# One float16 cast and one subtraction for two key tiles (1536 columns) in a block-sparse attention kernel

## The chip, the cores and the metric

The kernel runs on one core of one Trainium2 chip. The metric is the device time of one execution in microseconds (us). The kernel before was timed three times: 983.65, 980.24 and 983.49 us, median 983.49 us.

The engines are named as in the profile: PE (TensorE, matmuls) with PEld (its weight loads), DVE (VectorE), ACT (ScalarE), POOL (GpSimd), SP (SyncE, which issues every DMA of this kernel).

## The reference, cut to what matters

```python
scores = scale * np.matmul(q, k.transpose(0, 1, 3, 2))      # 4 x 8 heads, 768 tokens, 64 wide
...
scores = np.where(mask, scores, -1000000000.0)              # blocks of 32: window, ends, 3 sampled
scores = scores - np.max(scores, axis=-1, keepdims=True)
attn = np.exp(scores)
attn = attn / (np.sum(attn, axis=-1, keepdims=True) + 1e-09)
out = np.matmul(attn, v)
...
h = x @ w_in                                                # x: 3072 x 512, w_in: 512 x 2048
g = h - np.tanh(h)
return (g @ w_out).astype(np.float32)
```

## The kernel before, in words

The 32 heads are worked on in 16 pairs, as two heads fill 128 partitions. A head has six key tiles of 128 keys. Three pairs' worth of transposed q and k stand in three slots of SBUF (slot0 to slot2).

For each head and key tile, the attention part does these steps:

- **smax**, two heads ahead: PE computes plain scores into a PSUM tile `sm`, DVE takes their row maximum (`mc`, L259). After six tiles PE turns the maxima (`pmt`, L264), DVE scales them (`nm`, L266), and a DMA puts them as a row into the slot, so that the next step's matmuls subtract them.
- **qk_exp**: PE computes the scores of all 768 queries against 128 keys into a PSUM tile `st` (L283, L284); ACT writes their exponential into an SBUF tile `pe` (L287).
- **split**: the exponential becomes two float16 parts. `ph` is the cast of `pe` (on ACT, L297, or on DVE, L295); `pl` is `pe - ph` (on POOL or DVE, L299).
- **accum**: PE multiplies `ph` and `pl` with the values' two parts into a PSUM tile `av` (L313, L321, L322; 18 matmuls per tile). The two tiles of a pair of key tiles (0 and 1, 2 and 3, 4 and 5) are accumulated one behind the other, and the first is ordered behind the subtraction of the second.
- **norm**: DVE divides by the row sums (L331, L334, L335).

Once per pair of heads, **prep_qk** prepares a later pair: PE transposes k and q into PSUM tiles `ptk` and `ptq`, ACT writes the high parts `hik`, `hiq` (L200), DVE the low parts `lok`, `loq` (L201), and DMAs spread them into a slot (L213). **prep_v** splits the values (`am`, `pa`, `sb`, then `vhl` on ACT L240 and DVE L241). This falls into the odd heads. The PSUM tiles `st`, `sm`, `ptk` and `ptq` share three buffers (`big`); `av`, `pa` and `pmt` share two others. The feed-forward part follows from about 434 us on and is not touched.

All steps are written as events with a time in units of key tiles, sorted by it. A scheduler then makes each engine's order and hands out the buffers by its own estimate of when they come free, so durations that it expects change both. From head 5 on, `in_order` fixes the order of the `st`, `sm` and `av` matmuls on PE.

`load_pre` and `convert_pre` load six weight tiles (`raw...`, tag `wraw`, two buffers) during the attention, convert them on DVE (`cvti`, `cvto`; L436, L439, L442) and store them to DRAM (`wi`, `wo`).

Which casts and subtractions go to DVE stands in small tables by the tile's number modulo 12: casts 4 and 10, subtraction 11, and in the last heads casts 0, 2, 4, 6, 8, 10 and subtractions 2, 5, 8, 11. `pe` has four buffers, `ph` and `pl` eight each.

Of the kernel before, what the change touches and what calls it, by code (L numbers as in the profile page):

```python
# [11 lines left out]
F32 = mybir.dt.float32  # L12
# [10 lines left out]
P = 128  # L23
# [20 lines left out]
NV = 3  # L44
PH_DVE_END = (0, 2, 4, 6, 8, 10)
TF, NMH = 2, 2
TV0 = -4
PAIR = 0.99
PB = 8
XF = 8  # L50
# [8 lines left out]
RS, RQ, RV, HR = 1, 2.5, 3, 6  # L59
PL_DVE = (11,)  # L60
PL_DVE_END = (2, 5, 8, 11)
PH_DVE = (4, 10)

# [43 lines left out]
def attention(ctx, tc, q, k, v, samp, w_in, w_out, blocks, xscr, ident, ps, slots, wt, f2, ffn):  # L107
# [44 lines left out]
    def setup():  # L152
# [17 lines left out]
        nc.vector.tensor_scalar(out=neg[R, :], in0=allow, scalar1=1.0, scalar2=-MASKED, op0=ALU.subtract, op1=ALU.mult)  # L170
        nat = p2.tile([P, S], F32, tag="pe", name="nat", bufs=4)
        mk = p2.tile([P, S], F32, tag="pe", name="mk", bufs=4)
        nc.vector.tensor_copy(
# [102 lines left out]
    def qk_exp(h, kt):  # L276
# [8 lines left out]
        in_order(h, ms[0], ms[-1])  # L285
        pe = p2.tile([P, S], F32, tag="pe", name=f"pe{h}_{kt}", bufs=4)
        nc.scalar.activation(out=pe, in_=st[:, 0:S], func=AF.Exp, scale=0.125)  # L287
        pes[h, kt] = pe

    def split(h, kt):  # L290
        pe = pes.pop((h, kt))
        ph = p2.tile([P, S], F16, tag="ph", name=f"ph{h}_{kt}", bufs=PB)
        pl = p2.tile([P, S], F16, tag="pl", name=f"pl{h}_{kt}", bufs=PB)
        if (h * T + kt) % 12 in (PH_DVE if h < HPH else PH_DVE_END):
            nc.vector.tensor_copy(out=ph, in_=pe)  # L295
        else:
            nc.scalar.activation(out=ph, in_=pe, func=AF.Copy)  # L297
        eng = nc.vector if (h * T + kt) % 12 in (PL_DVE if h < HPL else PL_DVE_END) else nc.gpsimd
        d = eng.tensor_tensor(out=pl, in0=pe, in1=ph, op=ALU.subtract)  # L299
        plin[h, kt] = d  # L300
        phs[h, kt] = ph, pl

# [47 lines left out]
    def at(time, f, *args):  # L350
        ev.append((time, len(ev), f, args))
# [24 lines left out]
    def load_pre(m, ft):  # L376
        wraw[m, ft] = p2.tile([P, 1024], I32, tag="wraw", name=f"raw{m}{ft}")
        d = load_w(nc, wraw[m, ft], w_in, w_out, m, ft)
        if ft == 0:
            after(2, d)  # L380
# [7 lines left out]
    for h in range(2 * NPAIR):  # L388
        tsm = TSM + ramp(h, RS)
        for t in range(T):  # L390
            i = 6 * h + t
            at(i + tsm, smax, h, t)
            at(i, qk_exp, h, t)
            at(i + LSP, split, h, t)
            at(i + LAV + PAIR * (1 - t % 2), accum, h, t)
# [289 lines left out]
```

## Time and profile before

| What | Value |
|---|---|
| time, three runs | 983.65, 980.24, 983.49 us; median 983.49 us |
| profiled execution | span 983.2 us; its trace gives no other time |
| busy share of the span | PE 94%, PEld 78%, DVE 75%, ACT 64%, POOL 47% |
| exponentials on ACT (L287) | 192, mean 805 ns |
| casts on ACT (L297), on DVE (L295) | 154, mean 844 ns; 38, mean 704 ns |
| subtractions on POOL, on DVE (L299) | 173, mean 1692 ns; 19, mean 1455 ns |
| PE's wait for the exponential (st L283 <- ACT pe L287) | 13.4 us in 15 waits |

The exponentials run from 33.5 to 428 us of the span. Two heads take 23.5 us there: an even head some 10.5 and an odd one some 13.1. A row of a timeline has the start in us, the length in us, the engine, the line, the operation, output<-inputs, the count, and in brackets the idle time ahead of it with what ended it. A row of waits has who waited for whom, the sum in us, the number of waits and the longest.

### The profile page before, as it was taken

The page shows a single profiled execution, that of the slowest core. Times are in us where ns is not written, and L with a number is a line of the kernel's source. Part 1 is how long each engine was busy: PE and PEld are TensorE (multiplying, and loading weights), DVE is VectorE, ACT ScalarE, POOL GpSimd, SP SyncE. Part 2 cuts the span into 40 slices and gives each one's busy share as a digit, 9 for nine tenths or more (in the row PEclk, how much of TensorE's full clock was granted, in tenths as well). Part 3 has the DMA queues.
Part 4 walks back from the last instruction along what each step waited for, and adds up shares of the span by engine and source line. Part 5 has one row for each costly group of instructions (what it writes and reads, how often), then busy time and mean ns, then how long its engine had stood idle before and what let it go on. Part 6 is the DMA issues. An engine that isn't in the chain of part 4 may idle for free.

```text
span 983.2 us, 18548 instructions
## 1 busy us (share of the span) xinstructions
PE 922.6 (94%) x7264; PEld 771.1 (78%) x7264; DVE 733.4 (75%) x1119; ACT 629.7 (64%) x943; POOL 458.3 (47%) x308
## 2 busy tenths in 40 slices
PE   5788999999999999888999999999999999999997
PEld 3577788887888878767788888888888888888885
DVE  4589888887887878859999876765676666566664
ACT  1476888888888878656666665555555465555553
POOL 1365877777777777754445422222222222222221
PEclk9698999999999999898999999999999999999999
DMA  8796777676676667114451220210020000001001
GB/s 231 185 274 190 195 175 175 162 174 162 168 173 162 162 161 189 45 48 157 148 168 50 65 76 11 97 33 12 1 75 1 1 33 11 1 1 44 1 1 43
DMA packets 56263, 99.78 MB, mean 101 GB/s; under 512 B 6008, under 2 KB 26680, under 8 KB 56176
## 3 DMA queue, kind: packets, MB, share of 16 engines
q1 hardware_dynamic: 56176, 98.60, 37.0%
q8 instruction: 57, 0.93, 0.4%
q14 instruction: 30, 0.25, 0.1%
HBM read 44.64 MB, written 15.20 MB: 61 GB/s over the span
## 4 chain that ended last, share of the span: by engine, by line
PE 77%; ACT 6%; DMA 5%; DVE 5%; issue 3%; SPq 1%; POOL 1%; ACTq 0%; POOLq 0%; DVEq 0%
PE pf L537 25%; PE pf L569 8%; PE pf L570 8%; PE pf L571 8%; PE st L283 6%; PE st L284 5%; PE sm L255 5%; ACT pe L287 3%; PE av L313 2%; PE av L321 2%; PE av L322 2%; DMA slot<-lok 2%; DMA slot<-nm 2%; DVE mc L259 1%; PE pf L451 1%
## 5 line engine op out<-in xcount | busy, mean ns | idle before, releaser
L299 POOL TENSOR_TENSOR pl<-pe,ph 128x768 f16<-128x768 f32 x173 | 290.0, 1692 | 130.5 <-ACT ph L297 67.5
L560 POOL TENSOR_TENSOR gl<-t,gh 128x512 fp32r<-128x512 f32 x96 | 124.0, 1292 | 358.4 <-ACT gh L559 307.0
L259 DVE TENSOR_REDUCE mc<-sm 128x1 f32<-128x768 f32 x192 | 181.0, 951 | 53.1 <-PE sm L255 49.2
L287 ACT ACTIVATE pe<-st 128x768 f32<-128x768 f32 x192 | 154.1, 805 | 78.4 <-PE st L284 68.5
L283 PE MATMUL st<-slot 128*128 128x512 f32 (+1 forms) x384 | 146.4, 382 | 17.1 <-ACT pe L287 13.4
L552 DVE TENSOR_TENSOR t<-t,pf 128x512 f32<-128x512 f32 x94 | 64.5, 686 | 123.3 <-ACT t L546 123.2
L559 ACT ACTIVATE gh<-t 128x512 fp32r<-128x512 f32 x96 | 60.6, 632 | 120.2 <-DVE t L556 120.2
L297 ACT ACTIVATE ph<-pe 128x768 f16<-128x768 f32 x154 | 130.0, 844 | 4.7
L284 PE MATMUL st<-slot 89*128 89x512 f32 (+1 forms) x384 | 126.1, 349 | 1.0 <-DMA slot<-nm 1.0
L313 PE MATMUL av<-vhl,ph 128*128 128x65 f16 x1152 | 120.7, 195 | 0.0
L322 PE MATMUL av<-vhl,pl 128*128 128x65 f16 x1152 | 119.6, 194 | 0.9 <-POOL pl L299 0.9
L255 PE MATMUL sm<-slot 88*128 88x512 f32 (+1 forms) x384 | 111.1, 376 | 9.6 <-DMA slot<-hiq 7.0
L321 PE MATMUL av<-vhl,ph 128*128 128x64 f16 x1152 | 119.7, 196 | 0.0
L313 PEld LDWEIGHTS <-ph 128*128 128x128 f16 x1152 | 106.6, 97 | 13.6 <-issue 12.9
L322 PEld LDWEIGHTS <-pl 128*128 128x128 f16 x1152 | 107.9, 100 | 3.0 <-issue 1.5
L321 PEld LDWEIGHTS <-ph 128*128 128x128 f16 x1152 | 107.9, 98 | 0.7 <-issue 0.5
L544 ACT ACTIVATE u<-pf 128x512 f32<-128x512 f32 x94 | 56.2, 598 | 80.5 <-PE pf L537 80.2
L283 PEld LDWEIGHTS st<-slot 128*128 128x128 f32 x384 | 74.9, 195 | 35.1 <-ACT pe L287 18.5
L284 PEld LDWEIGHTS st<-slot 89*128 89x128 f32 x384 | 75.5, 197 | 11.2 <-DMA slot<-nm 2.2
L255 PEld LDWEIGHTS sm<-slot 88*128 88x128 f32 x384 | 62.6, 202 | 17.0 <-DMA slot<-mk 6.3
L570 PE MATMUL pf<-wx,gh 128*128 128x512 f32 x192 | 74.7, 389 | 0.0
L569 PE MATMUL pf<-wx,gh 128*128 128x512 f32 x192 | 74.7, 389 | 0.0
(123 smaller groups left out, 1962.8 us busy)
## 6 DMA issues: line engine op xcount, KB each, us to landing
slot<-hik SPq DMA_DIRECT2D x64, 192.0 KB
slot<-hiq SPq DMA_DIRECT2D x64, 192.0 KB
stage<-w_in SPq DMA_DIRECT2D x13, 512.0 KB
stage<-w_out SPq DMA_DIRECT2D x13, 512.0 KB
rawk<-k SPq DMA_DIRECT2D x16, 384.0 KB
rawq<-q SPq DMA_DIRECT2D x16, 384.0 KB
slot<-lok SPq DMA_DIRECT2D x32, 192.0 KB
slot<-loq SPq DMA_DIRECT2D x32, 192.0 KB
```

The source lines that it names most:

```text
L255: nc.tensor.matmul(pm[:, c], lhsT=sB[s][0:88, j, t * P : (t + 1) * P], rhs=sA[s][0:88, j, c], start=True, stop=True)
L259: maxed.append(nc.vector.tensor_reduce(out=mcs[h][:, t : t + 1], in_=pm[:, 0:S], op=ALU.max, axis=AX.X))
L283: ms.append(nc.tensor.matmul(st[:, c], lhsT=sC[s][:, j, kc], rhs=sD[s][:, j, c], start=True, stop=False))
L284: ms.append(nc.tensor.matmul(st[:, c], lhsT=sA[s][0:89, j, kc], rhs=sB[s][0:89, j, c], start=False, stop=True))
L287: nc.scalar.activation(out=pe, in_=st[:, 0:S], func=AF.Exp, scale=0.125)
L299: d = eng.tensor_tensor(out=pl, in0=pe, in1=ph, op=ALU.subtract)
L313: m = nc.tensor.matmul(o[:, t, :], lhsT=ph[:, c], rhs=vv[:, 0:65], start=(kt == 0 and t == 0), stop=False, skip_group_check=True)
L321: nc.tensor.matmul(o[:, t, 0:64], lhsT=ph[:, c], rhs=vv[:, 65:129], start=False, stop=False, skip_group_check=True)
L322: m = nc.tensor.matmul(o[:, t, :], lhsT=pl[:, c], rhs=vv[:, 0:65], start=False, stop=last, skip_group_check=True)
L537: nc.tensor.matmul(h, lhsT=w[:, cc], rhs=x[:, c, :], start=(k == 0), stop=(k == 3 * NCT - 1))
L569: nc.tensor.matmul(o, lhsT=gh[:, c], rhs=wo[0][ft], start=(ft == f0), stop=False)
L570: nc.tensor.matmul(o, lhsT=gh[:, c], rhs=wo[1][ft], start=False, stop=False)
```

## The change

Two key tiles share one `pe` tile of 1536 columns: two exponentials write its halves, and one cast and one subtraction read it whole. `ph` and `pl` get 1536 columns as well; `accum` reads their halves with the same matmuls as before. `split` is called for odd tiles alone.

The tables now count pairs of tiles modulo 6: DVE casts pair 2 (the last of an even head), and no subtraction until the last two heads, where it has pairs 1 and 5; in the last heads DVE casts pairs 0, 2 and 4. In columns the casts on DVE are as many as before; the subtraction of one tile in twelve moves from DVE to POOL. `pe` has three buffers of 1536 for four of 768, `ph` and `pl` four for eight; `wraw` has one for two.

```diff
-PH_DVE_END = (0, 2, 4, 6, 8, 10)
+PH_DVE_END = (0, 2, 4)
...
-PB = 8
+PB = 4
+NPE = 3
...
-PL_DVE = (11,)
-PL_DVE_END = (2, 5, 8, 11)
-PH_DVE = (4, 10)
+PL_DVE = ()
+PL_DVE_END = (1, 5)
+PH_DVE = (2,)
...
-        nat = p2.tile([P, S], F32, tag="pe", name="nat", bufs=4)
-        mk = p2.tile([P, S], F32, tag="pe", name="mk", bufs=4)
+        nat = p2.tile([P, S], F32, tag="pe", name="nat", bufs=NPE)
+        mk = p2.tile([P, S], F32, tag="pe", name="mk", bufs=NPE)
...
-        pe = p2.tile([P, S], F32, tag="pe", name=f"pe{h}_{kt}", bufs=4)
-        nc.scalar.activation(out=pe, in_=st[:, 0:S], func=AF.Exp, scale=0.125)
-        pes[h, kt] = pe
+        if kt % 2 == 0:
+            pes[h, kt // 2] = p2.tile([P, 2 * S], F32, tag="pe", name=f"pe{h}_{kt}", bufs=NPE)
+        nc.scalar.activation(out=pes[h, kt // 2][:, kt % 2 * S : (kt % 2 + 1) * S], in_=st[:, 0:S], func=AF.Exp, scale=0.125)
 
     def split(h, kt):
-        pe = pes.pop((h, kt))
-        ph = p2.tile([P, S], F16, tag="ph", name=f"ph{h}_{kt}", bufs=PB)
-        pl = p2.tile([P, S], F16, tag="pl", name=f"pl{h}_{kt}", bufs=PB)
-        if (h * T + kt) % 12 in (PH_DVE if h < HPH else PH_DVE_END):
+        pe = pes.pop((h, kt // 2))
+        ph = p2.tile([P, 2 * S], F16, tag="ph", name=f"ph{h}_{kt}", bufs=PB)
+        pl = p2.tile([P, 2 * S], F16, tag="pl", name=f"pl{h}_{kt}", bufs=PB)
+        n = (h * T + kt) // 2 % 6
+        if n in (PH_DVE if h < HPH else PH_DVE_END):
             nc.vector.tensor_copy(out=ph, in_=pe)
         else:
             nc.scalar.activation(out=ph, in_=pe, func=AF.Copy)
-        eng = nc.vector if (h * T + kt) % 12 in (PL_DVE if h < HPL else PL_DVE_END) else nc.gpsimd
+        eng = nc.vector if n in (PL_DVE if h < HPL else PL_DVE_END) else nc.gpsimd
         d = eng.tensor_tensor(out=pl, in0=pe, in1=ph, op=ALU.subtract)
-        plin[h, kt] = d
-        phs[h, kt] = ph, pl
+        for x in range(2):
+            plin[h, kt - 1 + x] = d
+            phs[h, kt - 1 + x] = ph[:, x * S : (x + 1) * S], pl[:, x * S : (x + 1) * S]
...
-        wraw[m, ft] = p2.tile([P, 1024], I32, tag="wraw", name=f"raw{m}{ft}")
+        wraw[m, ft] = p2.tile([P, 1024], I32, tag="wraw", name=f"raw{m}{ft}", bufs=1)
...
-            at(i + LSP, split, h, t)
+            if t % 2:
+                at(i + LSP, split, h, t)
```

The changed program's lines stand one to four lower (L255 is now L256, L287 is L289, L331 is L334).

The scheduler makes another order of it. Names in the rows below are tile, head or pair, key tile and a running number; `st19_4` is the score tile of head 19 and key tile 4, `sm21_2` the one for the maxima of head 21, `hik11` the high part of k of pair 11. All odd heads from 7 to 27 read alike.

On DVE, in the odd head 19, before:

```order
L259 TENSOR_REDUCE mc21_4748<-sm21_0_4749 128x1
L235 TENSOR_SCALAR sb10_4679<-sb10_4679 128x1
L266 TENSOR_SCALAR nm20_4702<-pmt20_4700 6x128
L238 TENSOR_SCALAR sb10_4679<-sb10_4679 128x1
L259 TENSOR_REDUCE mc21_4748<-sm21_1_4777 128x1
L201 TENSOR_TENSOR lok11_4758<-ptk11_4759,hik11_4757 128x768
L241 SCALAR_TENSOR_TENSOR vhl1_104<-rawv10_3711,sb10_4679,vhl1_104 128x12x64
L331 SCALAR_TENSOR_TENSOR rs18_4822<-av18_4615,sb9_4207 128x6
L334 RECIPROCAL rs18_4822<-rs18_4822 128x6
L259 TENSOR_REDUCE mc21_4748<-sm21_2_4850 128x1
```

and now:

```order
L260 TENSOR_REDUCE mc21_4462<-sm21_0_4463 128x1
L233 TENSOR_REDUCE sb10_4394<-pa10_4392 128x1
L236 TENSOR_SCALAR sb10_4394<-sb10_4394 128x1
L239 TENSOR_SCALAR sb10_4394<-sb10_4394 128x1
L202 TENSOR_TENSOR lok11_4468<-ptk11_4469,hik11_4467 128x768
L260 TENSOR_REDUCE mc21_4462<-sm21_1_4486 128x1
L267 TENSOR_SCALAR nm20_4416<-pmt20_4414 6x128
L334 SCALAR_TENSOR_TENSOR rs18_4531<-av18_4334,sb9_3952 128x6
L242 SCALAR_TENSOR_TENSOR vhl1_104<-rawv10_3490,sb10_4394,vhl1_104 128x12x64
L337 RECIPROCAL rs18_4531<-rs18_4531 128x6
L260 TENSOR_REDUCE mc21_4462<-sm21_2_4559 128x1
```

The low part lok11 moved ahead of the maximum over sm21_1, and nm20 behind it; between that maximum and the one over sm21_2 there stand now nm20, rs18, vhl1 and the reciprocal.

On PE, at the end of the same odd head, with the semaphores that each row waits for (the engine that signals is in the name), before:

```order
L255 MATMUL sm21_2_4850<-slot1_74 128x512 [waits DVE_49]
L255 MATMUL sm21_2_4850<-slot1_74 128x256
L283 MATMUL st19_5_4867<-slot0_73 128x512 [waits Activation_49]
L284 MATMUL st19_5_4867<-slot0_73 128x512
L283 MATMUL st19_5_4867<-slot0_73 128x256
L284 MATMUL st19_5_4867<-slot0_73 128x256
L255 MATMUL sm21_3_4874<-slot1_74 128x512 [waits DVE_49]
```

and now:

```order
L256 MATMUL sm21_2_4559<-slot1_74 128x512 [waits DVE_49]
L256 MATMUL sm21_2_4559<-slot1_74 128x256
L284 MATMUL st19_5_4572<-slot0_73 128x512 [waits DVE_49]
L285 MATMUL st19_5_4572<-slot0_73 128x512
L284 MATMUL st19_5_4572<-slot0_73 128x256
L285 MATMUL st19_5_4572<-slot0_73 128x256
L256 MATMUL sm21_3_4578<-slot1_74 128x512 [waits Activation_49]
```

The order of the matmuls is the same; the buffers are not. By the program's addresses st19_5 stood in the buffer of st19_4 (freed by ACT's exponential), and stands now in that of sm21_2 (freed by DVE's maximum); sm21_3 now takes the buffer of st19_4.

On SP, in the first heads, before:

```order
L267 DMA slot1_74<-nm2_475 1x6x128
L145 DMA rawk4_871<-k 128x768
L145 DMA rawq4_873<-q 128x768
L213 DMA slot2_75<-hik2_571 64x768 x2
L213 DMA slot2_75<-hiq2_584 64x768 x2
```

and now:

```order
L268 DMA slot1_74<-nm2_459 1x6x128
L146 DMA rawk4_830<-k 128x768
L386 DMA wi0_76<-cvti0_1794 128x512
L146 DMA rawq4_832<-q 128x768
L214 DMA slot2_75<-hik2_546 64x768 x2
L214 DMA slot2_75<-hiq2_559 64x768 x2
```

The store of the first converted weight tile (wi0), which waits for DVE's conversion, moved ahead of the load of q of pair 4 and of the DMAs that fill slot2.

## The prediction

> **What bounds the kernel now.** I read the windows by stage first, then the waits of TensorE, then the timeline around the wait that repeats.
>
> ```profile
> 33.00:106.00 73.00, 64.76 (x720) 53.92 (x720) 60.74 (x90) 50.28 (x63) 48.19 (x27) 0.88 0.79 224
> 106.00:382.00 276.00, 261.54 (x3479) 225.48 (x3475) 227.28 (x349) 229.50 (x290) 208.51 (x128) 1.00 0.67 165
> 382.00:434.00 52.00, 47.12 (x655) 40.80 (x653) 39.95 (x58) 37.66 (x53) 39.73 (x23) 0.93 0.31 85
> ```
>
> Columns: stretch, length, then busy time of PE, PEld, DVE, ACT and POOL, the granted clock, the DMA share. The change touches these three stretches alone; the feed-forward part behind 434 us runs none of its lines. In the long middle one PE is busy 95% of the time and no other engine over 84%. Time saved on ACT, DVE or POOL there is worth only the PE waits that it ends, 14.5 us at the most, and the waits view says which.
>
> ```profile
> PE st L283 <- ACT pe L287: 10.9, 12, 0.9
> PE sm L255 <- ACT pe L287: 2.4, 2, 1.4
> ```
>
> This is the window 110 to 380 us. Twelve times, once in every odd head, PE waits 0.9 us; the rest is two single waits. One of the twelve:
>
> ```profile
> 280.16 0.51 PE L255 MATMUL sm<-slot 88*128 88x512 f32 x2
> 281.61 0.50 PE L283 MATMUL st<-slot 128*128 128x512 f32 x1 [0.94 <-ACT pe L287]
> ...
> 276.96 0.79 ACT L200 ACTIVATE hik<-ptk 128x768 fp32r<-128x768 f32 x1
> 277.65 0.94 ACT L240 ACTIVATE vhl<-rawv,sb 128x768 f16<-128x768 f32 x1
> 278.49 0.79 ACT L287 ACTIVATE pe<-st 128x768 f32<-128x768 f32 x1
> 279.31 0.84 ACT L297 ACTIVATE ph<-pe 128x768 f16<-128x768 f32 x1
> 280.06 0.79 ACT L200 ACTIVATE hiq<-ptq 128x768 fp32r<-128x768 f32 x1
> 280.75 0.80 ACT L287 ACTIVATE pe<-st 128x768 f32<-128x768 f32 x1
> ```
>
> Score tile 5 of the odd head stands in the PSUM buffer of tile 4, whose exponential comes last in a full ACT queue and ends at 281.55.
>
> **The casts on ACT.** A cast of 1536 is not in the trace, so its price is bounded.
>
> ```profile
> L297 ACT ACTIVATE ph<-pe 128x768 f16<-128x768 f32 x154 | 130.0, 844 | 4.7
> L559 ACT ACTIVATE gh<-t 128x512 fp32r<-128x512 f32 x96 | 60.6, 632 | 120.2 <-DVE t L556 120.2
> ```
>
> From 512 to 768 columns the time grows by 212 ns, 0.83 ns a column; 768 more columns make 844 + 636 = 1480 ns. The ends are 844 (the single cast) and 1688 (twice it). I take 1480, the value on the line through both rows: 77 casts for 154 save 77 x 208 ns = 16 us of ACT. In even heads PE is busy throughout, so this hides behind PE. In odd heads ACT no longer sets the wait, as follows.
>
> **The odd head's wait, which stays.** The rows of the program's order above show that tile 5 (st19_5) now waits for DVE: its buffer is that of sm21_2, the matmul just ahead of it, and the maximum over that tile must end first.
>
> ```profile
> 275.69 0.82 PE L198 MATMUL ptk<-ident,rawk 128*128 128x128 f32 x6
> ...
> 276.83 0.27 DVE L266 TENSOR_SCALAR nm<-pmt 6x128 fp32r<-6x128 f32 x1
> ...
> 277.73 0.96 DVE L259 TENSOR_REDUCE mc<-sm 128x1 f32<-128x768 f32 x1 [0.57 <-PE sm L255]
> 278.60 0.95 DVE L201 TENSOR_TENSOR lok<-ptk,hik 128x768 fp32r<-128x768 f32 x1
> 279.46 1.01 DVE L241 SCALAR_TENSOR_TENSOR vhl<-rawv,sb,vhl 128x768 f16<-128x768 f32 x1
> 280.39 0.15 DVE L331 SCALAR_TENSOR_TENSOR rs<-av,sb 128x6 f32<-128x6 f32 x1
> 280.58 0.19 DVE L334 RECIPROCAL rs<-rs 128x6 f32<-128x6 f32 x1
> 280.70 0.96 DVE L259 TENSOR_REDUCE mc<-sm 128x1 f32<-128x768 f32 x1
> ```
>
> The maximum cannot start before sm21_2 ends at 280.67, so it ends at 281.66 and tile 5 starts at 281.72 at best: 0.1 us later than now. DVE may also come late. Its new queue has lok, the maximum of sm21_1, nm (0.27), rs, vhl, the reciprocal and then this maximum. With hik ending at 277.35 (the transposes of k end at 276.5, then 0.79), the durations add up to 277.4 + 0.95 + 0.96 + 0.27 + 0.15 + 1.01 + 0.19 = 280.93, and to 280.45 with the 0.08 us by which neighbours overlap in these rows. So the wait grows by 0.1 to 0.3 us; I take 0.15, as the overlap is what the rows show: 12 x 0.15 = **+1.8 us** (1.2 to 3.6). The merge gains nothing here because the scheduler, given other durations, hands out other buffers. The two single waits of 2.4 us I leave as they are (-2.4 to +2.4).
>
> The maxima's transpose (pmt20) also moves, from ahead of tile 3 into the weighted sum behind it, and with it nm20 and its DMA, which SP now issues behind the four of hik.
>
> ```profile
> 277.12 0.76 SPq L267 DMA_DIRECT2D slot<-nm  x1
> 278.00 2.44 SPq L213 DMA_DIRECT2D slot<-hik  x4
> ...
> 284.96 0.81 ACT L287 ACTIVATE pe<-st 128x768 f32<-128x768 f32 x1 [0.58 <-PE st L284]
> ```
>
> The matmul that reads it is done by 284.96 and starts some 0.8 us before. Now the issue ends 6 us ahead of that; then hik's four run from 277.4 to 279.8, nm ends at 280.6, and 3.5 us are left. No row shows a landing that needs more in this stretch, so I cost it at nothing; each excess over 3.5 us would be paid twelve times.
>
> **The casts on DVE, the subtractions, and the pair's longer chain.**
>
> ```profile
> L299 POOL TENSOR_TENSOR pl<-pe,ph x173: 1637/1652/2360, 35.2 to 430.0; 128x768 f16<-128x768 f32 x173
> L299 DVE TENSOR_TENSOR pl<-pe,ph x19: 936/1522/2231, 64.0 to 429.9; 128x768 f16<-128x768 f32 x19
> L295 DVE CAST ph<-pe x38: 545/550/1257, 46.0 to 428.8; 128x768 f16<-128x768 f32 x38
> ...
> 263.01 0.79 ACT L287 ACTIVATE pe<-st 128x768 f32<-128x768 f32 x1
> ...
> 269.80 0.19 PE L322 MATMUL av<-vhl,pl 128*128 128x65 f16 x1
> ```
>
> Minimum, median and maximum in ns. For 1536 columns POOL takes between 1.65 us (the single one) and 4.72 (twice the longest); I take twice the median, 3.30, since no POOL row of this kind shows a fixed part. A DVE cast lies between 0.55 and 2.51, taken 1.10, and a DVE subtraction between 0.94 and 4.46, taken 2.9 (twice the mean of 1455). In steady state the chain has room: a pair's second exponential ends at 263.80 at the latest, plus 1.48 plus 3.30 is 268.6, and PE reads the low part at 269.80, so 1.2 us is spare. POOL holds six of them per two heads, 19.8 us in 23.5, and the three double buffers turn over well after. The cover is gone if POOL needs over 4.5 us. The one subtraction in twelve that DVE gave up (1.5 us per two heads) ended nobody's wait in the list of PE above, so it gains nothing either. Cost: nothing, and no gain.
>
> **The last two heads** have no maxima to pace PE.
>
> ```profile
> 421.24 1.59 ACT L287 ACTIVATE pe<-st 128x768 f32<-128x768 f32 x2 [0.16 <-PE st L284]
> ...
> 423.93 1.51 ACT L287 ACTIVATE pe<-st 128x768 f32<-128x768 f32 x2 [0.23 <-PE st L284]
> ```
>
> A pair takes 2.7 us. Three pairs in a row now go to POOL, 3 x 3.30 = 9.9 us against 8.1 for PE: up to 1.8 late, some of it hidden by the h matmuls that stand ahead of the last pairs. I take **+1.5 us** (0 to 4; the upper end has the DVE subtraction at 4.46 ahead of the cast that the first of the three needs).
>
> **The first heads.**
>
> ```profile
> PE st L283 <- DVE mc L259: 2.2, 3, 1.0
> PE pmt L264 <- DVE mc L259: 2.1, 3, 1.5
> PE st L283 <- DVE lok L201: 1.2, 1, 1.2
> ...
> 56.26 1.18 SPq L213 DMA_DIRECT2D slot<-hik  x2
> ...
> 58.05 0.67 DVE L442 SCALAR_TENSOR_TENSOR cvti<-rawi,cvti 128x512 int32<-128x512 int32 x1
> ```
>
> Here (30 to 110 us) PE waits 5.5 us for DVE, which the weight conversions crowd. With one wraw buffer each conversion waits for the one before, so two of the six move past these heads, and the DVE's subtractions go to POOL. That can end all 5.5 us. Against it, SP now holds the store of cvti0 ahead of the DMAs of hik2: they went out at 56.26, and the conversion ended at 58.72 (58.05 + 0.67), so they can be 2.5 us late. The setup tiles nat and mk share the three buffers of pe; the third pair's exponential is the first that could need theirs, and what that costs lies within these ends. Neither end is shown; between -5.5 and +2.5 I take the middle, **-1.5 us**.
>
> **Sum.** -1.5 + 1.8 + 1.5 = +1.8 on the profiled execution's 983.2 us (its span; the trace has nothing of it outside) makes 985.0. The median of the runs is 983.49, 0.3 above that span, which I leave out. **985 us, no change**; its own range is 979 to 988. About 0.5%, 4.9 us, is what a measurement of this kernel can tell from no change.
>
> **Rivals.** *First heads freed* (0.25): the 5.5 us of DVE waits go, the single waits of 2.4 go, the end costs nothing: 983.2 - 7.9 + 1.2 = 976.5. For it speaks that DVE is the named releaser; against it the SP queue.
>
> *Nothing saved by width* (0.14): the wide cast costs 1.69. Two casts per even head then end 0.2 us after the next score tile is ready, and the maximum matmul that reuses its buffer waits: 12 x 2 x 0.2 = 4.8 us, which with 1.8 and 2.5 at the end makes 992. It decides from about 1.6 us. The Trainium skill, page "Perfetto Trace Analysis", section "Optimizing Scalar/DVE Operations", speaks for this side: it says that where Scalar or Vector are not saturated but cause bubbles elsewhere, breaking instructions up may let work finish sooner; by it the widening itself is wrong here, and the trace agrees so far as ACT has 46 us idle in the middle stretch.
>
> *DVE collides with POOL* (0.11): the instruction at L241 has run longer in some places.
>
> ```profile
> L241 DVE SCALAR_TENSOR_TENSOR vhl<-rawv,sb,vhl x16: 1006/1009/2018, 39.4 to 402.3; 128x768 f16<-128x768 f32 x16
> ```
>
> It now stands ahead of the maximum that frees tile 5. If a POOL subtraction is still running when it starts near 279.4, it can take 2.02 instead of 1.01: 12 x 1.0 = 12 us, 997. With 3.30 on POOL the pair's subtraction ends near 279.0, so it decides from about 3.7 us. The Trainium skill, page "SBUF — State Buffer", section "Who interferes with whom", gives the reason: a DVE instruction with two SBUF inputs and a GpSimd one that reads SBUF share a port pair that one holds for its whole length.
>
> That the merge is not made as said is excluded: the built program has 77 ACT and 79 POOL instructions fewer.
>
> **Numbers.** The forecast has 0.50. Faster 0.25 (first heads freed), within 0.5% 0.50, slower 0.25 (both others). The unknown bounds give 983.2 - 5.5 - 2.4 + 1.2 = 976.5 and 983.2 + 2.5 + 3.6 + 2.4 + 4 = 995.7; the range is 976 to 996.
>
> **What would show it.** The twelve waits of st must be named for DVE mc with 1.0 to 1.2 us; if they are gone, the buffers' step is wrong. ACT's cast must show near 1480 ns and POOL's 2700 to 3400. Waits of av for pl in the middle would refute the spare 1.2 us. A wait of st for slot<-nm would show the moved DMA late. The first stretch tells whether conversions or the SP queue counted.

## The result, and the profile after

| | median | runs |
|---|---|---|
| before | 982.19 us | 4, from 980.24 to 983.65 |
| after | 1006.93 us | 4, from 1004.68 to 1008.06 |

The change makes the kernel slower: the ratio is 1.0248, with a 95% interval of 1.0223 to 1.0273, or 24.7 us between the medians. The profiled execution has a span of 1006.3 us, 23.1 more than before.

First, groups of instructions of the changed kernel, from the page: line, engine, operation, tiles, count, then busy us, mean ns, and the idle time ahead of them with what ended it.

```profile
L301 POOL TENSOR_TENSOR pl<-pe,ph 128x1536 f16<-128x1536 f32 x94 | 293.2, 3124 | 149.2 <-ACT ph L299 94.6
L284 PE MATMUL st<-slot 128*128 128x512 f32 (+1 forms) x384 | 147.7, 385 | 24.3 <-DVE mc L260 20.6
L285 PE MATMUL st<-slot 89*128 89x512 f32 (+1 forms) x384 | 127.9, 353 | 5.1 <-DMA slot<-nm 5.1
```

The subtraction takes 3.12 us, near the 3.30 that was taken. The scores (L284) now wait 20.6 us for a maximum. About half of that is the wait of the odd heads that was foreseen, as the waits view from 110 to 382 us shows (sum, count, longest):

```profile
PE st L284 <- DVE mc L260: 16.3, 12, 2.9
```

Ten of these twelve are 1.05 us each; the other two, 2.9 and 2.8, lie in the first heads. To find where the 23 us go, the span is cut where the same work is done: from the first exponential of head 0 to the first of head 8, from there to the start of the last exponential, and the rest. The windows before (length, then busy time of PE, PEld, DVE, ACT and POOL, granted clock, DMA share):

```profile
33.50:142.30 108.80, 98.08 (x1147) 82.45 (x1147) 91.64 (x138) 80.72 (x101) 76.25 (x44) 0.92 0.73 204
142.30:427.30 285.00, 268.85 (x3587) 232.02 (x3586) 232.07 (x351) 233.13 (x298) 215.64 (x133) 0.99 0.63 155
427.30:983.20 555.90, 540.45 (x2488) 445.25 (x2484) 394.05 (x603) 311.31 (x541) 161.74 (x124) 0.99 0.14 47
```

and after:

```profile
31.80:162.70 130.90, 105.69 (x1148) 88.93 (x1148) 97.46 (x130) 77.37 (x82) 72.20 (x23) 0.86 0.66 171
162.70:449.60 286.90, 266.96 (x3579) 231.16 (x3577) 223.38 (x323) 223.88 (x241) 223.75 (x74) 0.99 0.63 154
449.60:1006.30 556.70, 540.77 (x2490) 446.06 (x2490) 396.15 (x602) 311.50 (x541) 160.69 (x124) 0.99 0.15 47
```

The first eight heads take 22.1 us more, everything else together 1.0 more (1.9 + 0.8, and 1.7 less ahead of them). In those heads PE does the same matmuls. It stands idle for 25.2 us instead of 10.7 (130.90 - 105.69 against 108.80 - 98.08), which is 14.5 of the 22.1. The other 7.6 are matmuls that run longer, at a mean granted clock of 0.86 instead of 0.92.

Now what PE waits for there. The timeline of DVE and of POOL (the last three rows) around 83 to 97 us:

```profile
83.00 2.95 DVE L446 SCALAR_TENSOR_TENSOR cvto<-rawo,cvto 128x512 int32<-128x512 int32 x1
85.87 1.81 DVE L260 TENSOR_REDUCE mc<-sm 128x1 f32<-128x768 f32 x2
...
93.56 3.52 DVE L446 SCALAR_TENSOR_TENSOR cvti<-rawi,cvti 128x512 int32<-128x512 int32 x1
97.01 0.28 DVE L233 TENSOR_REDUCE sb<-pa 128x1 f32<-128x128 f32 x1
...
82.30 3.10 POOL L301 TENSOR_TENSOR pl<-pe,ph 128x1536 f16<-128x1536 f32 x1 [3.10 <-DVE ph L297]
85.83 3.10 POOL L301 TENSOR_TENSOR pl<-pe,ph 128x1536 f16<-128x1536 f32 x1 [0.44 <-ACT ph L299]
93.43 3.10 POOL L301 TENSOR_TENSOR pl<-pe,ph 128x1536 f16<-128x1536 f32 x1 [4.50 <-ACT ph L299]
```

A conversion step that takes 0.68 us by itself takes 2.95 and 3.52 us. Each began while a subtraction ran on POOL and ended 0.55 us behind that subtraction's end (85.95 against 85.40, 97.08 against 96.53). The maximum and `sb` stand behind it in DVE's queue, and PE waits for them; for the maximum it is this row:

```profile
86.87 0.50 PE L284 MATMUL st<-slot 128*128 128x512 f32 x1 [2.88 <-DVE mc L260]
```

Other DVE instructions are held too: L242 takes 3.56 us at 37.79 and 2.89 us at 68.12, for 1.00 in all the later heads, and PE waits 2.45 and 2.00 us behind it.

The other kind of wait, on DVE at 143 us, with SP's rows that led to it (last two):

```profile
138.03 0.96 DVE L260 TENSOR_REDUCE mc<-sm 128x1 f32<-128x768 f32 x1
143.29 0.43 DVE L440 TENSOR_SCALAR cvto<-rawo 128x512 int32<-128x512 int32 x1 [4.30 <-DMA rawo<-w_out]
...
144.46 0.92 DVE L260 TENSOR_REDUCE mc<-sm 128x1 f32<-128x768 f32 x1
...
136.40 0.44 SPq L386 DMA_DIRECT2D wi<-cvti  x1
136.88 0.45 SPq L432 DMA_DIRECT2D rawo<-w_out  x1
```

The one raw buffer is free only when the conversion before has read it (its last step ends at 125.74 us). By then SP has the store and the load behind a pair's DMAs, and the load goes out at 136.88. DVE reaches the conversion at 138.99, stands still for 4.30 us, and the maximum that PE needs is behind it (PE waits 2.83 us, to 145.43). The whole stretch has three such waits for rawo:

```profile
DVE cvto L440 <- DMA rawo<-w_out: 7.2, 3, 4.3
```

So there are two theories. **Q**: with one raw buffer DVE's queue is blocked by conversions whose weights came late. **C**: the wider subtraction on POOL holds DVE's conversion steps for longer. The rival of both is that the wide cast, the shared tiles or the scheduler's new order do it.

### The profile page after: what moved, and what is told of

Its sections match the earlier page's. It is cut to its first block, busy times and chain, and to the rows that moved or that the text cites. A ratio compares the mean times of both kernels' runs of the same rounds, so it can differ in the third digit from the quotient of the medians.

```text
span 1006.3 us, 18198 instructions
## 1 busy us (share of the span) xinstructions
PE 929.0 (92%) x7264; PEld 777.7 (77%) x7264; DVE 732.5 (73%) x1083; ACT 617.3 (61%) x866; POOL 461.4 (46%) x229
## 4 chain that ended last, share of the span: by engine, by line
PE 79%; DVE 8%; DMA 6%; issue 2%; ACT 2%; SPq 1%; POOL 1%; DVEq 0%; POOLq 0%; ACTq 0%
PE pf L541 25%; PE pf L573 8%; PE pf L574 8%; PE pf L575 8%; PE st L284 6%; PE sm L256 6%; PE st L285 5%; PE av L316 3%; PE av L325 3%; PE av L324 3%; DVE mc L260 2%; DMA slot<-nm 2%; DMA rawo<-w_out 2%; PE ptk L199 1%; PE pf L455 1%
## 5 line engine op out<-in xcount | busy, mean ns | idle before, releaser
L301 POOL TENSOR_TENSOR pl<-pe,ph 128x1536 f16<-128x1536 f32 x94 | 293.2, 3124 | 149.2 <-ACT ph L299 94.6
L289 ACT ACTIVATE pe<-st 128x768 f32<-128x768 f32 x192 | 154.7, 809 | 109.5 <-PE st L285 107.8
L284 PE MATMUL st<-slot 128*128 128x512 f32 (+1 forms) x384 | 147.7, 385 | 24.3 <-DVE mc L260 20.6
L316 PE MATMUL av<-vhl,ph 128*128 128x65 f16 x1152 | 126.2, 198 | 4.5 <-DVE sb L233 2.7
L324 PE MATMUL av<-vhl,ph 128*128 128x64 f16 x1152 | 125.3, 198 | 2.5 <-DVE vhl L242 2.5
L325 PE MATMUL av<-vhl,pl 128*128 128x65 f16 x1152 | 123.7, 196 | 1.9 <-POOL pl L301 1.9
L316 PEld LDWEIGHTS <-ph 128*128 128x128 f16 x1152 | 109.3, 99 | 14.2 <-issue 12.9
L256 PE MATMUL sm<-slot 88*128 88x512 f32 (+1 forms) x384 | 111.5, 377 | 6.5 <-DMA slot<-hiq 5.2
L299 ACT ACTIVATE ph<-pe 128x1536 f16<-128x1536 f32 x77 | 114.1, 1482 | 2.0
L324 PEld LDWEIGHTS <-ph 128*128 128x128 f16 x1152 | 110.4, 100 | 5.1 <-issue 4.8
L325 PEld LDWEIGHTS <-pl 128*128 128x128 f16 x1152 | 110.2, 102 | 4.3 <-POOL pl L301 2.6
L284 PEld LDWEIGHTS st<-slot 128*128 128x128 f32 x384 | 76.0, 198 | 42.4 <-DVE mc L260 26.3
L256 PEld LDWEIGHTS sm<-slot 88*128 88x128 f32 x384 | 63.9, 206 | 16.0 <-issue 5.6
```

The lines of the kernel that those rows point to most:

```text
L256: nc.tensor.matmul(pm[:, c], lhsT=sB[s][0:88, j, t * P : (t + 1) * P], rhs=sA[s][0:88, j, c], start=True, stop=True)
L284: ms.append(nc.tensor.matmul(st[:, c], lhsT=sC[s][:, j, kc], rhs=sD[s][:, j, c], start=True, stop=False))
L289: nc.scalar.activation(out=pes[h, kt // 2][:, kt % 2 * S : (kt % 2 + 1) * S], in_=st[:, 0:S], func=AF.Exp, scale=0.125)
L316: m = nc.tensor.matmul(o[:, t, :], lhsT=ph[:, c], rhs=vv[:, 0:65], start=(kt == 0 and t == 0), stop=False, skip_group_check=True)
L324: nc.tensor.matmul(o[:, t, 0:64], lhsT=ph[:, c], rhs=vv[:, 65:129], start=False, stop=False, skip_group_check=True)
L325: m = nc.tensor.matmul(o[:, t, :], lhsT=pl[:, c], rhs=vv[:, 0:65], start=False, stop=last, skip_group_check=True)
```

## The experiments

Ratios are to the kernel before, run beside each on the same chip, with 95% intervals. "First heads" is the stretch from the first exponential of head 0 to that of head 8 in the profiled execution (108.8 us before, 130.9 after). That is one execution of each kernel: e15 and e18, whose sources differ in the last two heads alone, took 107.9 and 110.0 us there, so some 2 us say nothing.

### Taking away Q, C and both (e1 to e3)

e1 gives the raw weights two buffers again, without more SBUF, in tiles that lie idle:

```diff
-        wraw[m, ft] = p2.tile([P, 1024], I32, tag="wraw", name=f"raw{m}{ft}", bufs=1)
+        wraw[m, ft] = ffn.stage[m == "o"]
```

> The changed kernel, but the raw weights go by turns into the two tiles stage0 and stage1, which lie idle until the feed-forward part, so that there are two buffers for them again. Theory Q (one raw buffer: DVE stands in its queue at a conversion whose weights were loaded late, 8.6 us in five waits for rawo and rawi, and maxima stand behind it): most of the loss comes back, 988 to 992 us, and no wait of DVE for rawo over 2 us ahead of a maximum. Theory C (collision: a DVE instruction that reads two SBUF tiles is held for as long as POOL's subtraction runs, which is now 3.1 us and not 1.65): the loss stays, 1002 to 1008 us, and conversions still show rows of 2 to 3.5 us. Both at once: 995 to 1001.

e2 halves the subtraction and nothing else:

```diff
-        d = eng.tensor_tensor(out=pl, in0=pe, in1=ph, op=ALU.subtract)
         for x in range(2):
-            plin[h, kt - 1 + x] = d
+            c = slice(x * S, (x + 1) * S)
+            plin[h, kt - 1 + x] = eng.tensor_tensor(out=pl[:, c], in0=pe[:, c], in1=ph[:, c], op=ALU.subtract)
```

> The changed kernel, but each subtraction is given as two of 768 columns; the exponentials' tile and the cast stay at 1536, and there is one raw buffer. Theory C: the longest a DVE instruction is held falls from 2.9 to about 1.6 us; the four PE waits of 2.5 to 2.9 us behind held rows (41.4, 86.9, 97.3 and 120.3 us) shrink or go, 995 to 1000 us. Theory Q: no change, 1004 to 1008 us, as the waits for rawo stay.

e3 has both diffs.

> Both edits: two raw buffers (in stage0 and stage1) and subtractions of 768. If Q and C explain the loss between them: 983 to 988 us. If something else of the change does it (the cast of 1536, three pair tiles for four single ones, the order that the scheduler makes of it): 993 us or more.

| | median us | ratio | interval | first heads |
|---|---|---|---|---|
| after | 1006.93 | 1.0248 | 1.0223 to 1.0273 | 130.9 |
| e1, two raw buffers | 998.89 | 1.0172 | 1.0131 to 1.0212 | 124.7 |
| e2, halves | 999.24 | 1.0174 | 1.0125 to 1.0222 | 128.5 |
| e3, both | 991.21 | 1.0088 | 1.0053 to 1.0122 | 117.4 |

Each takes away some 8 us (0.76% and 0.74%) and both together 16 (1.60%), so that within the noise they add up. e1 came out where "both at once" had it and e2 where theory C had it. The first heads give e1 6.2 us, and the halves on top of it, e3, another 7.3. In e2's profiled execution, the longest of its four (1003.52 us), they show 2.4 us alone, so that C's price rests on e2's median and on the step from e1 to e3. In e1 the held rows stay:

```profile
83.16 2.95 DVE L446 SCALAR_TENSOR_TENSOR cvti<-stage,cvti 128x512 int32<-128x512 int32 x1
86.03 3.31 DVE L440 TENSOR_SCALAR cvto<-stage 128x512 int32<-128x512 int32 x1
```

In e2 the held rows shrink and the waits for rawo stay, in that execution 14.5 us in three, one of them much longer:

```profile
110.32 0.43 DVE L440 TENSOR_SCALAR cvto<-rawo 128x512 int32<-128x512 int32 x1 [6.79 <-DMA rawo<-w_out]
...
113.13 1.48 DVE L446 SCALAR_TENSOR_TENSOR cvto<-rawo,cvto 128x512 int32<-128x512 int32 x1
```

e3 fell between what was expected of it by Q and C alone (983 to 988) and by something else alone (993 or more): about 9 us were left.

### Q alone, on the kernel before (e4)

```diff
-        wraw[m, ft] = p2.tile([P, 1024], I32, tag="wraw", name=f"raw{m}{ft}")
+        wraw[m, ft] = p2.tile([P, 1024], I32, tag="wraw", name=f"raw{m}{ft}", bufs=1)
```

> The kernel before, with one raw buffer for two and nothing else changed. Theory Q: slower by 10 us or more, 993 to 1000 us, with DVE waits for rawo ahead of maxima. Theory C: 982 to 986 us, as POOL's subtractions are 1.65 us.

990.34 us, ratio 1.0098 (1.0057 to 1.0138): 8.6 us more, less than Q expected and as much as e1 gave back. The same waits appear, here with subtractions of 768 (DVE, three rows):

```profile
70.85 0.86 DVE L436 TENSOR_SCALAR cvto<-rawo 128x512 int32<-128x512 int32 x1 [3.25 <-DMA rawo<-w_out]
...
99.22 0.60 DVE L436 TENSOR_SCALAR cvto<-rawo 128x512 int32<-128x512 int32 x1 [1.91 <-DMA rawo<-w_out]
...
127.26 0.43 DVE L436 TENSOR_SCALAR cvto<-rawo 128x512 int32<-128x512 int32 x1 [3.35 <-DMA rawo<-w_out]
```

So what the one raw buffer costs is shown from both sides. The way is not the one of theory Q everywhere, though. In the first two of these three places PE itself waits for the row `nm`, 2.90 and 1.51 us, whose DMA SP issued right behind that of the late weights:

```profile
63.18 0.44 SPq L428 DMA_DIRECT2D rawo<-w_out  x1
64.00 0.75 SPq L267 DMA_DIRECT2D slot<-nm  x1
...
71.06 0.80 PE L284 MATMUL st<-slot 89*128 89x512 f32 x1 [2.90 <-DMA slot<-nm]
```

Only behind the third does PE wait for maxima (1.73 and 1.32 us). How the 8.6 us divide between the two ways isn't shown.

### The rest: width, engine or tiles (e5, e13, e14)

e5 keeps the shared tiles and e1's two raw buffers, but gives casts and subtractions per tile again, with the engines' tables of the kernel before:

```diff
+        c = slice(kt % 2 * S, (kt % 2 + 1) * S)
+        pe, ph, pl = pe[:, c], phs[h, kt // 2, 0][:, c], phs[h, kt // 2, 1][:, c]
...
-PH_DVE = (2,)
+PH_DVE = (4, 10)
...
-            if t % 2:
-                at(i + LSP, split, h, t)
+            at(i + LSP, split, h, t)
```

> What is left of the loss after the raw buffers and the subtractions, some 9 us. This kernel has the change's shared tiles (three of pe, four of ph and pl) and two raw buffers in stage0 and stage1, but every cast and subtraction is of 768 columns again, given per tile, with the engines' tables of before. Theory W (the cast of 1536 starts only when the pair's second exponential is done, and DVE has both of its casts in the even head): 980 to 985 us. Theory B (the fewer, larger buffers and the order that comes with them): 988 to 993 us.

987.36 us, ratio 1.0027 (0.9992 to 1.0061). The ten runs spread from 979 to 995 and the median lies between what the two theories had, so this didn't decide it. e13 is e3 with each cast given as halves, at the same place and on the same engines:

```diff
+        for x in range(2):
+            c = slice(x * S, (x + 1) * S)
             if n in (PH_DVE if h < HPH else PH_DVE_END):
-                nc.vector.tensor_copy(out=ph, in_=pe)
+                nc.vector.tensor_copy(out=ph[:, c], in_=pe[:, c])
             else:
-                nc.scalar.activation(out=ph, in_=pe, func=AF.Copy)
+                nc.scalar.activation(out=ph[:, c], in_=pe[:, c], func=AF.Copy)
```

> Two raw buffers, subtractions of 768, and now also each cast as two of 768, on the same engines and at the same place as in the change (both behind the pair's second exponential, pair 2 of six on DVE). 991 us with the wide cast. If the cast's width makes the rest (a wide DVE cast holds up a maximum longer): 983 to 987 us. If it is the place (both casts behind the second exponential, both DVE casts in the even head) or the tiles and the order: 989 to 993 us.

985.49 us, ratio 1.0034 (1.0008 to 1.0061), against 1.0088 for e3. So 0.54%, some 5 us, belong to the cast's width. The two intervals just touch, but the first heads say the same: 110.0 us instead of e3's 117.4. Also the odd heads' waits are for the exponential again (0.94 us), so the scheduler hands out the buffers as before once it sees narrow casts. e14 is e3 with no DVE cast until the last two heads:

```diff
-PH_DVE = (2,)
+PH_DVE = ()
```

> Two raw buffers, subtractions of 768, casts of 1536, but all casts on ACT until the last two heads, none on DVE. If the rest of the loss is DVE, which the first heads crowd: 982 to 987 us, and no PE wait named for DVE over 1.3 us but where conversions stand. If it is not: 990 to 996 us, as ACT gets 1.48 us more per two heads and the odd heads' exponential may come later.

992.42 us, ratio 1.0102 (1.0066 to 1.0137), first heads 121.3 us: no better than e3. So it doesn't help to take the wide cast off DVE; that it costs as much on ACT in its place isn't excluded. How the width acts in the first heads, through its latency or through the order that the scheduler makes of it, stays open. Nor was the 0.3% that e13 leaves traced further.

### The conversions out of the first heads (e6 to e8)

Both theories act through conversions that stand ahead of maxima. These three kernels (the changed one, the one before, and e3) tie each conversion behind a maximum, so that the six fall into heads 6 to 27:

```diff
+        def late(d):
+            tc.add_manual_dep(
+                d.ins, maxed[-1].ins.name, mybir.DependencyInfo(mybir.DependencyClass.NoSync, mybir.DependencyReason.DATA), reason="late"
+            )
...
-        nc.sync.dma_start(out=wt[m, ft], in_=convert(nc, f2, wraw[m, ft], f"cvt{m}{ft}"))
+        nc.sync.dma_start(out=wt[m, ft], in_=convert(nc, f2, wraw[m, ft], f"cvt{m}{ft}", late=late))
```

> The changed kernel with one raw buffer and subtractions of 1536, but each of the six weight conversions is tied behind the maximum that stands ahead of it in the events, so that they fall into the heads from 6 to 27 and not into the first eight. If Q and C both act through the conversions in the first heads: the stretch from the first exponential of head 0 to that of head 8 falls from 130.9 us to 112 to 120 (108.8 before the change), and the six conversions cost up to 3 us each where they now stand, 990 to 1002 us in all. If the loss isn't brought by conversions, the stretch stays above 125 us.

> The kernel before with the six conversions tied behind the maxima in the same way. If the conversions are also what the kernel before loses in its first heads: its stretch from head 0 to head 8 falls from 108.8 us to 100 to 105, and the whole is 975 to 983 us, depending on what the conversions cost in the later heads. If they are no burden with two buffers and short subtractions: 983 to 992 us.

> The changed kernel with two raw buffers in stage0 and stage1, subtractions of 768 and the conversions tied behind the maxima: the cast of 1536 and the shared tiles are what is left of the change. If the rest of the loss also came through the conversions: 977 to 984 us and a stretch from head 0 to head 8 of 102 to 108 us. If it is the wide cast or the buffers: 986 to 992 us, stretch 112 us or more.

| | median us | ratio, interval | first heads |
|---|---|---|---|
| e6, after | 1001.34 | 1.0180 (1.0115 to 1.0244) | 111.2 |
| e7, before | 994.12 | 1.0113 (1.0061 to 1.0164) | 110.7 |
| e8, e3 | 994.39 | 1.0123 (1.0067 to 1.0180) | 110.4 |

In the changed kernel the first heads fall from 130.9 to 111.2 us, with wide casts and subtractions and one raw buffer:

```profile
32.50:143.70 111.20, 98.26 (x1148) 82.85 (x1147) 87.24 (x117) 76.94 (x81) 71.79 (x23) 0.92 0.65 166
```

That is all but 2.4 us of the loss, and the clock is 0.92 again. (e6's profiled run took 993.8 us, 7.5 below its median; e8 and, below, e15 show the same in runs near theirs.) So the loss there does come through the conversions with their loads and stores, that of the wide cast too. For the kernel before it brought nothing in the first heads, against the 100 to 105 us expected. The totals of e7 and e8 lie above everything that was expected of them. The conversions now stand in odd heads, where DVE has the low parts, and PE waits up to 3.2 us in one piece for a maximum there.

### Even heads, and PSUM for the intermediate tile (e9 to e12)

Here each of the three steps of a conversion is tied behind a maximum of its own, in even heads:

```diff
-W0, DW = 40, 24.7
+W0, DW, DC = 45, 24, 1
...
-        at(W0 + DW * x + 4, convert_pre, "io"[x % 2], x // 2)
+        for y in range(3):
+            at(W0 + DW * x + 4 + DC * y, convert_pre, "io"[x % 2], x // 2)
```

> The changed kernel (one raw buffer, subtractions of 1536), with the six conversions in even heads from head 8 on, each of their three steps tied behind a maximum of its own (key tiles 1, 2, 3). Theory C: POOL runs some 19 of the 23.5 us of two heads, so that most steps that read two SBUF tiles are held, rows up to 3.5 us, and heads 8 to 28 take 243 to 250 us (241.5 with the change as it was); in all 988 to 1000 us. If the later cost in the runs with late conversions came only from their place in the odd heads, where DVE has the low parts: 239 to 242 us there, and 983 to 987 us in all.

e10 changes only where the intermediate tile stands:

```diff
-            steps[m, ft] = convert_steps(nc, f2, wraw[m, ft], f"cvt{m}{ft}", None, late)
+            steps[m, ft] = convert_steps(nc, f2, wraw[m, ft], f"cvt{m}{ft}", one(f"cp{m}{ft}"), late)
```

> The same, but the conversion's intermediate tile stands in PSUM (a buffer of those for av, pa and pmt, idle then), so that no step reads two SBUF tiles. Theory C: no conversion row over 1 us, heads 8 to 28 in 239 to 242 us, heads 0 to 8 in 107 to 112 us, in all 980 to 987 us: the change without its loss. If rows are held all the same, POOL's subtraction isn't what holds them through SBUF, and the times are those of the run without PSUM.

e11 and e12 are the same two edits on the kernel before.

> The kernel before (subtractions of 768, two raw buffers) with the conversions in even heads. Theory C: rows held up to 2.3 us, heads 8 to 28 in 241 to 247 us (239.2 before), in all 980 to 990 us.

> The kernel before with the conversions in even heads and their intermediate tile in PSUM. Theory C: no held conversion rows, heads 8 to 28 in 238 to 240.5 us, heads 0 to 8 in 102 to 109 us (108.9 before), in all 974 to 983 us, perhaps the best of all. If conversions in the first heads cost the kernel before nothing: 983 to 986 us.

This pair measures C by itself. The conversion steps of e9, minimum, median and maximum in ns:

```profile
L456 DVE TENSOR_SCALAR cvto<-rawo x3: 2379/2393/2396, 194.2 to 395.0; 128x512 int32<-128x512 int32 x3
L462 DVE SCALAR_TENSOR_TENSOR cvto<-rawo,cvto x3: 2770/2775/2779, 197.4 to 398.1; 128x512 int32<-128x512 int32 x3
L468 DVE SCALAR_TENSOR_TENSOR cvto<-rawo,cvto x3: 675/676/676, 200.9 to 401.7; 128x512 int32<-128x512 int32 x3
```

and of e10, with the same subtractions running on POOL beside them:

```profile
L456 DVE TENSOR_SCALAR cpo<-rawo x3: 682/685/685, 194.7 to 399.8; 128x512 int32<-128x512 int32 x3
L462 DVE SCALAR_TENSOR_TENSOR cpo<-rawo,cpo x3: 682/685/686, 196.2 to 401.3; 128x512 int32<-128x512 int32 x3
L468 DVE SCALAR_TENSOR_TENSOR cvto<-rawo,cpo x3: 677/677/678, 198.2 to 403.3; 128x512 int32<-128x512 int32 x3
```

With the intermediate tile in PSUM no step is held; with it in SBUF two of three are, by up to 2.1 us. The third meets a subtraction as well, but began 0.05 us ahead of it, and there the subtraction takes 3.60 us for 3.12:

```profile
200.94 0.68 DVE L468 SCALAR_TENSOR_TENSOR cvto<-rawo,cvto 128x512 int32<-128x512 int32 x1
200.99 3.60 POOL L301 TENSOR_TENSOR pl<-pe,ph 128x1536 f16<-128x1536 f32 x1 [1.39 <-issue]
```

In the kernel before (e11), with subtractions of 768, the same three steps take up to 1.9, 1.27 and 1.27 us. That subtractions hold the conversion steps is shown, and that the hold grows with the subtraction's length.

The times followed only where the rows are held: e9 997.43 us (1.0159, 1.0119 to 1.0198) and e11 989.82 (1.0065, 1.0038 to 1.0093) lie in all where theory C had them. e10 with 1000.20 (1.0179, 1.0139 to 1.0218) and e12 with 1000.65 (1.0182, 1.0140 to 1.0224) missed by 13 us and more. They got a new wait, which was not foreseen (waits view of e10, 142 to 400 us):

```profile
PE st L285 <- DMA slot<-nm: 12.7, 5, 3.5
```

The conversion held one of the two small PSUM buffers just when `pmt` of the odd head's maxima needed it, so that `nm` and its DMA were late.

### The changed kernel without its loss (e15)

e15 is e10 with the conversions 1.5 key tiles later, behind that `pmt`:

```diff
-W0, DW, DC = 45, 24, 1
+W0, DW, DC = 46.5, 24, 1
```

> The changed kernel with subtractions and casts of 1536 and one raw buffer; conversions in even heads through PSUM, 1.5 key tiles later than in the run before, so that the maxima's transpose has its PSUM buffer first. Theory C with the reading that the late nm DMA in the run before came from that transpose: no conversion row over 1 us, no wait for slot<-nm over 1 us behind 110 us, heads 8 to 28 in 240 to 244 us, in all 984 to 990 us. If the waits for nm stay, they come from elsewhere: 997 to 1002 us.

985.04 us, ratio 1.0025 (0.9999 to 1.0051). Casts and subtractions are 1536 wide and there is one raw buffer, as in the change. The first heads:

```profile
32.00:139.90 107.90, 97.14 (x1149) 81.83 (x1148) 79.64 (x112) 76.92 (x81) 71.68 (x23) 0.92 0.67 169
```

23.0 us less than with the change as it was, and no conversion row over 0.7 us. In one such head `pmt` now runs at 192.31, ahead of the conversion's first step at 194.61; in e10 it ran at 200.51, behind the last one. Behind 142 us the waits for `nm` are gone but for two of 1.0 and 0.8 us. So where the merged instructions don't meet the conversions, what they cost is at most some 5 us, the upper end of the interval, and may be nothing.

### Towards a faster kernel (e16 to e18)

e16 gives the kernel before four raw buffers:

```diff
-        wraw[m, ft] = p2.tile([P, 1024], I32, tag="wraw", name=f"raw{m}{ft}")
+        wraw[m, ft] = ffn.stage[m == "o"] if ft % 2 else p2.tile([P, 1024], I32, tag="wraw", name=f"raw{m}{ft}")
```

> The kernel before with four raw buffers (its two, and stage0 and stage1 for the middle two weights). Theory Q: one buffer cost 8.6 us since DVE waits in its queue for raw tiles; with two it still waits 2.6 us once for rawi, so that four gain up to 3 us: 978 to 983 us. If packing the six conversions closer crowds DVE in those heads instead: 984 to 992 us.

989.03 us, ratio 1.0068 (1.0042 to 1.0094), first heads 113.4 us: slower. More buffers don't go on to gain. The middle two conversions now alternate between 70 and 76 us, and the first of them waits for the store that frees the converted tile:

```profile
70.24 0.43 DVE L436 TENSOR_SCALAR cvti<-stage 128x512 int32<-128x512 int32 x1 [4.18 <-DMA wi<-cvti]
```

`nm` stands behind it in DVE's queue, and PE waits 3.76 us for that. e17 is the kernel before with the conversions of e15.

> The kernel before with the conversions in even heads through PSUM at the later place. Theory C, by which the first heads of both kernels lose through conversions: heads 0 to 8 in 104 to 108 us (108.9 before), heads 8 to 28 in 238 to 241 us, in all 977 to 982 us against 982 for the kernel before. If the first heads wait for other things in their place (the DMA of nm, as in other runs with late conversions): 982 to 986 us.

981.94 us, ratio 1.0004 (0.9984 to 1.0025). The first heads gain 3.2 us (105.6), and heads 8 to 28 give 2.3 back. This is the kernel that differs from e15 by the change alone: 0.2% between their ratios, within the noise. e18 is e15 with halves for the subtractions of the last two heads:

```diff
+        parts = (slice(0, S), slice(S, 2 * S)) if h >= HPL else (slice(0, 2 * S),)
+        ds = [eng.tensor_tensor(out=pl[:, c], in0=pe[:, c], in1=ph[:, c], op=ALU.subtract) for c in parts]
```

> The changed kernel with the conversions as in e15, and the subtractions of the last two heads given as halves of 768. If the length of the subtractions makes the wait there (DVE's took 4.09 us beside POOL's of 3.09): the wait of av for pl falls from 2.3 us to under 1, in all 982 to 984.5 us (985.0 without). If the wait stays above 1.5 us, POOL's queue makes it: 984.5 to 986 us.

985.38 us, ratio 1.0032 (1.0008 to 1.0055): the waits of av for pl there make 3.1 us, the longest 1.6 (2.4 and 2.3 in e15), so halves don't end them. By the expectation that puts them down to POOL's queue, which no run tests by itself. None of the runs is faster than the kernel before.

## Why the prediction was wrong

**The step that failed** is the one on the first heads. It said that with one wraw buffer "two of the six move past these heads" and that this "can end all 5.5 us" of DVE waits, with at most 2.5 us lost to SP's queue, and took -1.5. The first heads cost 22.1 us (20.4 from the span's start). The conversions did move: before, all six lie in heads 0 to 3, now three of them in heads 4 to 7. But each kept its place ahead of maxima in DVE's queue, and in that place two things went wrong:

- The load behind the one buffer comes late, and DVE waits for it in order (7.2 us in three waits, the longest 4.3). This is Q, 8 us by e1 and 8.6 by e4. The prediction counted the SP queue as a delay of one pair's DMAs, not as a delay of a load that DVE is stuck behind, nor of an `nm` issued behind that load (e4).
- A held conversion step lasts until POOL's subtraction is done, which now takes 3.1 us. This is C, some 8 us by e2 and by the step from e1 to e3. The prediction had this mechanism as a rival, but placed it at L241 in the odd heads, "from about 3.7 us". There it didn't occur: the new L242 runs at 1.00 us in those heads, as the prediction's sum had it, since POOL has just finished (in one head POOL's subtraction ends at 180.32, L242 runs from 181.25 to 182.25, and the next subtraction begins at 182.24). It occurred at the conversions and at the first two L242 (3.56 and 2.89 us). The sign was in the trace of before: the conversion's second step took up to 1.94 us there for 0.68, so it was held already, by the shorter subtraction.

```profile
L439 DVE SCALAR_TENSOR_TENSOR cvti<-rawi,cvti x3: 680/1301/1939, 55.3 to 85.8; 128x512 int32<-128x512 int32 x3
L446 DVE SCALAR_TENSOR_TENSOR cvti<-rawi,cvti x3: 680/2692/3521, 58.0 to 125.1; 128x512 int32<-128x512 int32 x3
```

(The first row is of the kernel before, second step; the other of the changed one, third step.) The Trainium skill, page "SBUF — State Buffer", section "Who interferes with whom", says that a DVE instruction with two SBUF inputs, or a tensor_scalar in a two-port mode, is blocked for the whole GpSimd instruction that got the ports first. The runs agree: held conversion steps end 0.28 to 0.55 us behind the subtraction, the step of e9 that came first isn't held, and with the tile in PSUM none is held.

These two make some 16 us of the loss. Of the other 9 some 5 belong to the cast's width (e13), by a way that stays open, and the rest wasn't traced.

The range of 976 to 996 missed, since its ends took these heads as worth 5.5 us at most. The rival that had DVE's waits there freed is refuted, and the one on the cast's price as well: the wide cast on ACT, which that rival put at 1.69 us, measured 1.482 against the 1.480 taken. The one on DVE, taken at 1.10, has a median of 1.60 and takes up to 2.96, as subtractions hold it too: the cast at 172.04 us ends at 173.71, behind a subtraction that runs from 169.78 to 172.90. Yet the cast's width costs some 5 us as long as the conversions stand in the first heads (e13), and when they don't (e15), no cost was measured, to within 5 us.

**The clock** added to all this. The prediction priced waits alone, but a third of the loss in the first heads (7.6 of 22.1 us) is matmuls that run slower. Two windows of the changed kernel show it around the 4.3 us wait; the last two rows are of another place:

```profile
140.00:145.00 5.00, 2.60 (x44) 2.12 (x42) 1.71 (x5) 1.62 (x2) 3.10 (x1) 1.00 0.48 184
145.00:150.00 5.00, 4.46 (x22) 3.36 (x23) 5.00 (x8) 1.73 (x3) 1.75 (x1) 0.60 0.42 131
...
120.29 0.50 PE L284 MATMUL st<-slot 128*128 128x512 f32 x1 [2.95 <-DVE mc L260]
...
120.00:125.00 5.00, 4.52 (x55) 3.94 (x55) 4.16 (x10) 1.62 (x2) 2.33 (x1) 1.00 0.67 192
```

In the first window PE is busy for 2.60 of 5 us; one idle time of 2.83 us reaches from it to 145.43, and in the next 5 us the granted clock is 0.60. The Trainium skill, page "TensorE: Matmul & The Clock Gate", section "What's actually happening", says that the clock falls to a half after an idle window of about 3.4 us. The rows agree that it falls after idle time, though here less than 3 us in one piece were enough. They weren't always: behind the 2.95 us ahead of 120.29 the granted clock stays at 1.00. What decides between the two isn't shown.

**The odd heads' wait** was right: it changed its name to DVE's maximum, and 1.05 us each lies within the 1.0 to 1.2 foreseen, and the way is the one foreseen, the buffer that DVE frees. The middle stretch has ten of the twelve. The two single waits, left open at 2.4 us either way, are gone there. The stretch takes 1.9 us more than before, and without the DMA below it would take some less.

**The moved nm DMA**, costed at nothing, was late once by more than 0.5 us. In the other odd heads its margin of 3.5 us held; in this one the DMA, issued from 276.68 to 277.98 us, lands just ahead of the matmul at 284.42 that waits for it:

```profile
276.68 1.30 SPq L268 DMA_DIRECT2D slot<-nm  x1
...
284.42 0.50 PE L285 MATMUL st<-slot 89*128 89x512 f32 x1 [3.27 <-DMA slot<-nm]
```

This is 3.3 us, paid once and not twelve times. Why it took so long there wasn't traced.

**The last two heads**, put at +1.5: from the start of the last exponential on, the span takes 0.8 us more, within the 0 to 4, and the wait that was foreseen is there (av for pl, 1.9 us in three). **POOL's chain** in the middle has its spare time as foreseen; no wait of av for pl appears there.

## What to carry to other kernels

Making an instruction longer on one engine can lengthen every hold that it puts on another. So look in the old trace for rows that already take two or three times their shortest, wherever they stand, and let their extra time grow with the new length. A buffer taken away to make room is a change of its own: ask which in-order queue will stand at the load that now comes later, and what stands behind it there, in the queue that issues the load too. Where PE's waits grow to 2 or 3 us, price the slower clock after them too.

## What the runs showed of the hardware

A conversion step from SBUF to SBUF on DVE that meets a subtraction on POOL waits for all the rest of it (2.39 us for 0.43 in the first step, 2.77 for 0.68 in the second), and the same steps through PSUM take 0.685 beside it. The first step, which has only one SBUF input, is held as well, which had not been counted on. Not every DVE instruction is: the row maximum `am`, read from SBUF, took 0.93 us at 120.16 in the middle of a subtraction (119.07 to 122.33). POOL's subtraction has little fixed cost: 1.65 us for 768 columns and 3.12 for 1536.
